# A routed two-layer kernel on one core: weight remainders on the matrix engine, a bf16 spreading product, and a token list stored as 16 rows

## The chip, the cores and the metric

The kernel runs on one core of a Trainium2 chip. The core's engines work side by side and meet at semaphores: TensorE (PE, matrix products into PSUM banks), VectorE (DVE), ScalarE (ACT), GpSimd (POOL), and SyncE (SP), which here only issues DMA transfers. Each engine takes its instructions in the order in which the program wrote them. The metric is the device time of one execution in microseconds.

## The reference, cut to what matters

```python
attn_out = _attn_ref(**attn_kwargs)            # banded local and global attention: B=4, H=8, S=544, D=64
x = attn_out.transpose(0, 2, 1, 3).reshape(B * S, H * D)      # 2176 tokens of 512
# routing: _moe_ref, E = 8 experts, cap = 2176 // 8 = 272
logits = x @ w_gate
order = np.argsort(-logits.flatten())
for idx in order:                              # the largest logit of all comes first
    tok, e = (int(idx) // E, int(idx) % E)
    if assigned[tok] >= 0 or counts[e] >= cap:
        continue
    assigned[tok] = e
    counts[e] += 1
for e in range(E):
    h = np.maximum(x[assigned == e] @ w1[e], 0.0)             # 512 -> 1024
    out[assigned == e] = h @ w2[e]                            # 1024 -> 512
# dense layer: _moe2_ref on all rows of out
h = x @ w_in                                                  # 512 -> 2048
P = a[0] + a[1] * h + a[2] * h**2 + a[3] * h**3
Q = 1.0 + np.abs(b[0]) * np.abs(h) + np.abs(b[1]) * h**2
return ((P / (Q + 1e-06)) @ w_out).astype(np.float32)         # 2048 -> 512
```

All tensors are float32 but w_in and w_out, which come as float64; the kernel reads those as pairs of 32-bit words and turns them into float32.

## The kernel before

The program has four kinds of work, and they overlap. First comes attention for the four batches, with the logits at its end; in between, the 32 pieces of 128x512 of w_in and w_out are loaded (SP) and turned into float32 (ScalarE and VectorE), all but the last four (NL), whose buffers come free later.

Then comes the routing, one turn for each expert. `search` finds the next expert that fills up: VectorE compares every token's best logit with 64 or 32 candidate thresholds (ind), TensorE counts (17 small bf16 products with oh), VectorE reduces the counts to one number per candidate (d), and TensorE spreads d over all 128 partitions by a product with an identity matrix, so that VectorE can choose the next candidates (nxt). This is done six times per expert (BITS) for seven experts; the eighth takes what is left. `members` then gives the chosen tokens slots, and two products (ha by rhs, spread by il) turn slots into a list of token numbers: il holds the list as 16 partitions of 17, idx as 128 partitions of 3. Before the change idx is also written to the DRAM tensor perm, 272 numbers of 4 bytes by three transfers. SP reads the expert's id (ei) into a register and loads the weights of this expert with it.

Third come the experts. GpSimd gathers the 272 rows of an expert from DRAM with three indirect transfers (t and p, later rows), TensorE transposes them, and ScalarE and VectorE split them into a high part, rounded to the fp32r format, and a low part, the remainder. All large products of the kernel are sums of three fp32r products (high by high, high by low, low by high, `mm3`). An expert's weights arrive in 16 loads of 256 KB (rows) and are split in the same way, the remainder by GpSimd, or for half of expert 0's by VectorE.

Last, the dense layer works on chunks of two or three blocks of 128 rows, 16 blocks of 128 hidden features each: `firsts` (into bank tq), `chain` (the quotient, on ScalarE and VectorE), `seconds` (into bank sc) and `store`, which reads the token numbers back from perm (ix) and writes the rows out with an indirect transfer. The dense weights need splitting once: `high` rounds a piece (ScalarE, whi_), and `low` makes the remainder (wlo_): two processes take pieces in turn, one on GpSimd, one on VectorE. Both begin as soon as the first piece is rounded, that is with the first routing.

The order on the engines is made at build time. Each piece of work is a generator that yields the engine and the time that it will hold it, or an event; the class Flow keeps a clock for each engine in a model and lets the process that can start first, or one of smaller rank shortly after, write its instructions next. The rank of `low` is 5 until the first expert is nearly there. Where TensorE would be idle before the first expert, `fill` writes products of ones by ones (`warm`), whose results nobody reads. So a change in one process moves the others as well.

Of the kernel before, what the change touches and what calls it, by code (L numbers as in the profile page):

```python
# [11 lines left out]
F32 = mybir.dt.float32  # L12
# [23 lines left out]
# turns a float64's high word, read as float32, into one whose exponent has float32's bias;  # L36
# what lies below 2^-119 becomes 0 or keeps below it
# [3 lines left out]
class Event:  # L41
    """Something that happens n times before the processes that wait for it go on."""
# [5 lines left out]
class Slots(Event):  # L48
    """n places, each taken by one process at a time."""
# [5 lines left out]
class Ring:  # L55
    """n buffers that are taken in turn. Who takes one gets the event of its release."""
# [9 lines left out]
class Flow:  # L66
    """The order in which the engines issue. A process is a generator; it yields (engine, time in us) and
    then traces the instructions that hold the engine for about that time, or yields an Event or Slots
    that it needs, or a time to pass; of a list of engines it gets the one that is free first, as
    self.engine. On a model of the engines' clocks the process that can start  # L70
    first goes on, or one of a smaller rank that follows shortly."""
# [75 lines left out]
    def free(self, e):  # L147
        """When an engine is free; the queue of the DMAs is kept short."""
        t = self.clock.get(e, 0.0)
        if e == "SP":  # L150
            queue = sum(p[3][0][1] for p in self.asks if p[3][0][0] == "DMA")
            t = max(t, self.clock.get("DMA", 0.0) + queue - QUEUE)
        return t
# [30 lines left out]
def moe_kernel(ctx: ExitStack, tc: tile.TileContext, q_l, k_l, v_l, q_g, k_g, v_g, w_gate, w1, w2,  # L184
               w_in, w_out, ca, cb, out, dbg=None):
    nc = tc.nc
# [29 lines left out]
    def warm(n, after=None):  # L216
        """Idle products: the array's clock stays up only while it is busy."""
# [12 lines left out]
    # 128 x 512 pieces of w_in (row block, column block) and of w_out (row block) in the order of use  # L230
# [14 lines left out]
    def load64(pool, i, v, bufs=2):  # L245
        """Steps that give a piece of a float64 tensor (its words as int32) as float32."""
# [10 lines left out]
    # ------------------------------------------------------------ attention  # L257
    vs, tail, tail_pe = [], [], []
    with ExitStack() as actx:
# [5 lines left out]
        # heads are taken in the order hh = 4 * (h % 2) + h // 2, pair pr holds hh = 2 pr and 2 pr + 1  # L265
# [9 lines left out]
        def copy(o, i):  # L275
            """A copy on the engine that the flow chose."""
            if flow.engine == "ACT":
                act(o, i, AF.Copy)
            else:
                V.tensor_copy(o, i)  # L280
# [14 lines left out]
        # band masks: partition (j, q), free (block of four, key)  # L295
# [9 lines left out]
        # dif[p, c] = key column - query in block, key column counted from the window's start  # L305
        nc.vector.tensor_scalar(dif, jq, pqf, -160.0, op0=OP.add, op1=OP.add)
        # keys lie in slots of 32, the global ones after every two blocks; a window of three blocks
        # and the global keys is four slots in a row, the global ones at place gp(its first block)
# [5 lines left out]
        def win(i):  # L314
            """The first block of the window of block i's queries."""
# [15 lines left out]
        # global q, k transposed: [(h2, d), pair, (b, s)]  # L331
# [24 lines left out]
        # ---- loads  # L356
# [22 lines left out]
        def load_two(src, b, r, slots, rows, name, ev):  # L379
            """256 rows, two neighbours in a partition."""  # L380
# [18 lines left out]
        def windows(b, half):  # L399
            """Window tiles: index n starts at key 32 n."""  # L400
# [34 lines left out]
        # ---- transposes of queries and keys  # L435
# [26 lines left out]
        def both_T(src, s, put, done, rank):  # L462
            """[(parity of the row, d), pair, row // 2] for each head of a pair."""
# [44 lines left out]
        def prep_q(b, r, rank):  # L508
            """Queries of eight blocks, block diagonal by head of a pair."""
# [11 lines left out]
        # ---- four blocks of 32 queries of all heads  # L521
# [32 lines left out]
        def tops_(u, ps, sc, A, mx, tops):  # L554
            # the scores and their largest, both times -scale
# [89 lines left out]
        def logits(XT, c):  # L645
# [9 lines left out]
            # [(j, e), tokens] -> [tokens, e], summed over j  # L655
# [8 lines left out]
        # ---- the 32 global queries of a batch against all 544 keys  # L664
# [119 lines left out]
        # ---- conversions of the dense layer's weights, between the others  # L784
# [53 lines left out]
    # ------------------------------------------------------------- routing  # L838
# [24 lines left out]
    ioi = rc.tile([128, 64], I32, name="ioi")  # L863
# [9 lines left out]
    # tri[p, m]: 1 for p < m, less 1 everywhere  # L873
    tri = rc.tile([128, 128], BF, name="tri")
    with tc.tile_pool(name="tmp", bufs=1) as tmp:
        wide = tmp.tile([128, 128], I32, name="wide")
        nc.gpsimd.iota(wide, pattern=[[1, 128]], base=0, channel_multiplier=0)
        widef = tmp.tile([128, 128], F32, name="widef")
        nc.vector.tensor_copy(widef, wide)
        nc.vector.tensor_scalar(tri, widef, pif, -1.0, op0=OP.is_gt, op1=OP.add)  # L880
    ones34 = rc.tile([128, 2 * NT], F32, name="ones34")
    nc.vector.memset(ones34, 1.0)
    # candidates: the first round's floats in sortable order, then bit patterns to flip
# [7 lines left out]
    # a float of 2^23 + v, v < 2^23, has the bits M23 + v: sums of steps give bit patterns  # L891
# [15 lines left out]
    # a one at column 128 - NS + p of partition p  # L907
# [3 lines left out]
    perm = dpool.tile([N, 1], I32, name="perm")  # L911

    # above every logit while a token is unassigned, then below every candidate
# [4 lines left out]
    # remaining places less a half  # L918
    REM = rc.tile([128, E], F32, name="REM")
    nc.vector.memset(REM, float(CAP) - 0.5)  # L920
    # tokens given to an expert so far | tokens tied at the threshold
# [710 lines left out]
```

## Time and the profile before

| | |
|---|---|
| time, median of 3 runs | 950.34 us (948.73 to 950.40) |
| span of the profiled execution | 948.0 us |
| busy: TensorE, VectorE, ScalarE, GpSimd | 856.5, 740.7, 498.9, 282.2 us |
| instructions | 20310 |

The span runs from the first instruction to the last one of the profiled execution; its own time outside the profiler is not among the three runs, whose median is 2.3 us above the span. Busy times of an engine are shares of the span and say nothing of where the engine was waited for; for this the span is cut into stretches, and the waits are read in each.

### The profile page before, as it was taken

How to read it: one execution, taken by the hardware profiler on the slowest of the kernel's cores; microseconds unless marked ns; L12 is line 12 of the kernel's file. 1: busy time of each engine (PE TensorE's matmuls, PEld its weight loads, DVE VectorE, ACT ScalarE, POOL GpSimd, SP SyncE). 2: the span in 40 equal slices, each digit the busy share in tenths (PEclk: the TensorE clock that was granted, in tenths of full speed). 3: DMA queues.
4: the chain of work that ended last, by engine and by line, in shares of the span. 5: the costliest groups of instructions: out<-in, count | busy, mean ns of one | idle time of the engine just before them, and what ended most of it. 6: DMA issues, size and time to landing. Idle time of an engine off the chain costs nothing.

```text
span 948.0 us, 20310 instructions
## 1 busy us (share of the span) xinstructions
PE 856.5 (90%) x7692; PEld 732.0 (77%) x7692; DVE 740.7 (78%) x1879; ACT 498.9 (53%) x1123; POOL 282.2 (30%) x229
## 2 busy tenths in 40 slices
PE   6879787856599699999999999999999999999997
PEld 4657665623279588888888889988899899899886
DVE  4657778889478498989879888988988757758985
ACT  5768867761043244554554455445455555646763
POOL 3111111055224132432434333252334343331001
PEclk8989888865779799999999999999999999999999
DMA  9999998620543421322122122212213313210000
GB/s 214 211 232 259 247 252 234 191 79 1 74 129 51 85 68 45 59 78 79 47 68 90 35 58 79 79 46 80 79 35 91 90 40 96 90 46 1 23 1 34
DMA packets 134194, 89.90 MB, mean 95 GB/s; under 512 B 31536, under 2 KB 122160, under 8 KB 134096
## 3 DMA queue, kind: packets, MB, share of 16 engines
q1 hardware_dynamic: 130672, 79.67, 32.3%
q0 software_dynamic: 2896, 8.92, 4.3%
q8 instruction: 60, 0.98, 0.6%
q14 instruction: 38, 0.31, 0.1%
q10 hardware_dynamic: 528, 0.02, 0.0%
HBM read 68.19 MB, written 8.92 MB: 81 GB/s over the span
## 4 chain that ended last, share of the span: by engine, by line
PE 62%; DVE 13%; issue 9%; DMA 9%; ACT 4%; SPq 2%; POOL 1%; POOLq 0%; DVEq 0%; ACTq 0%
PE sc L1174 7%; PE sc L1176 6%; PE sc L1175 6%; PE tq L1174 5%; PE sc L1179 5%; PE tq L1175 5%; PE tq L1176 5%; PE sc L1181 5%; PE sc L1180 5%; PE av L964 2%; PE sc L545 2%; DMA stg<-in_moe_w_out_dram 2%; DMA VW<-vr 1%; PE av L972 1%; DMA p<-xd,idx 1%
## 5 line engine op out<-in xcount | busy, mean ns | idle before, releaser
L1356 POOL TENSOR_TENSOR wlo<-rows,whi 128x512 fp32r<-128x512 f32 x120 | 174.3, 1454 | 368.4 <-ACT whi L1349 353.4
L1174 PE MATMUL tq<-yr,wh 128*128 128x256 f32 (+1 forms) x512 | 152.1, 297 | 1.4 <-DVE p L1493 1.4
L1175 PE MATMUL tq<-yr,wh 128*128 128x256 f32 (+1 forms) x512 | 148.8, 291 | 0.0
L1176 PE MATMUL tq<-yr,ws 128*128 128x256 f32 (+1 forms) x512 | 148.7, 290 | 0.0
L1174 PEld LDWEIGHTS tq<-yr,wh 128*128 128x128 f32 x512 | 97.4, 190 | 4.1 <-issue 2.1
L1179 PE MATMUL sc<-wh,t 128*128 128x512 f32 x248 | 99.7, 402 | 0.0
L1181 PE MATMUL sc<-wh,t 128*128 128x512 f32 x248 | 98.3, 397 | 0.4 <-DVE t L1521 0.4
L1175 PEld LDWEIGHTS tq<-yr,wh 128*128 128x128 f32 x512 | 97.6, 191 | 0.8
L1176 PEld LDWEIGHTS tq<-yr,ws 128*128 128x128 f32 x512 | 97.9, 191 | 0.0
L1180 PE MATMUL sc<-ws,t 128*128 128x512 f32 x248 | 97.6, 394 | 0.0
L1349 ACT ACTIVATE whi<-rows 128x512 fp32r<-128x512 f32 x120 | 75.5, 630 | 32.9 <-DMA rows<-in_moe_w_dram 25.3
L1388 ACT ACTIVATE hh<-sc 128x272 fp32r<-128x272 f32 x64 | 25.4, 396 | 118.5 <-PE sc L1176 118.3
L1481 ACT ACTIVATE t<-tq,coef 128x512 f32<-128x512 f32 (+1 forms) x67 | 44.8, 669 | 58.7 <-PE tq L1176 49.5
L1174 PE MATMUL sc<-xhi,whi 128*128 128x272 f32 x240 | 74.0, 308 | 0.0
L1174 PE MATMUL sc<-hh,whi 128*128 128x272 f32 x240 | 71.2, 296 | 0.0
L1176 PE MATMUL sc<-xhi,wlo 128*128 128x272 f32 x240 | 69.9, 291 | 0.0
L1175 PE MATMUL sc<-xlo,whi 128*128 128x272 f32 x240 | 69.7, 291 | 0.0
L1176 PE MATMUL sc<-hh,wlo 128*128 128x272 f32 x240 | 69.2, 288 | 0.0
L1175 PE MATMUL sc<-hl,whi 128*128 128x272 f32 x240 | 69.0, 288 | 0.0
L1499 DVE SCALAR_TENSOR_TENSOR t<-t,b 128x512 f32<-128x512 f32 (+1 forms) x67 | 50.8, 758 | 17.3 <-ACT t L1483 16.9
L1502 ACT ACTIVATE t<-t,cq 128x512 f32<-128x512 f32 (+1 forms) x67 | 47.3, 706 | 22.2 <-DVE t L1499 22.0
L1181 PEld LDWEIGHTS sc<-wh,t 128*128 128x128 f32 x248 | 46.5, 188 | 15.1 <-DVE t L1521 4.4
(289 smaller groups left out, 2191.1 us busy)
## 6 DMA issues: line engine op xcount, KB each, us to landing
rows<-in_moe_w_dram SPq DMA_DIRECT2D x128, 256.0 KB, 2.9
stg<-in_moe_w_in_dram SPq DMA_DIRECT2D x16, 512.0 KB, 4.9
stg<-in_moe_w_out_dram SPq DMA_DIRECT2D x16, 512.0 KB, 4.9
VW<-vr SPq DMA_DIRECT2D x24, 256.0 KB, 5.1
kr<-in_k_l_dram SPq DMA_DIRECT2D x8, 512.0 KB, 7.3
qr<-in_q_l_dram SPq DMA_DIRECT2D x8, 512.0 KB, 6.2
vr<-in_v_l_dram SPq DMA_DIRECT2D x16, 256.0 KB, 5.4
VW<-vr SPq DMA_DIRECT2D x32, 128.0 KB, 4.7
```

The lines of the kernel that those rows point to most:

```text
L1174: nc.tensor.matmul(ps, whi, xhi, start=first, stop=False)
L1175: nc.tensor.matmul(ps, whi, xlo, start=False, stop=False)
L1176: nc.tensor.matmul(ps, wlo, xhi, start=False, stop=last)
L1179: nc.tensor.matmul(ps, ghi, whi, start=first, stop=False)
L1180: nc.tensor.matmul(ps, ghi, wlo, start=False, stop=False)
L1181: nc.tensor.matmul(ps, glo, whi, start=False, stop=last)
L1349: nc.scalar.activation(hi, raw, AF.Copy)
L1356: (V if alt else nc.gpsimd).tensor_tensor(lo, raw, hi.bitcast(F32), op=OP.subtract)
L1388: nc.scalar.activation(hh, ph[:, :CAP], AF.Relu)
L1481: nc.scalar.activation(q, ph, AF.Abs, scale=b0)
L1499: V.scalar_tensor_tensor(q, r, b1, q, op0=OP.mult, op1=OP.add)
L1502: nc.scalar.activation(r, q, AF.Ln, bias=cq)
```

## The change

Three things are changed. First, until the first expert is known (the event routed[0]), the remainder of a dense piece is made by TensorE: an fp32 product of the identity by the float32 piece, and, added in the same PSUM bank, an fp32r product of the negative identity (neg) by the rounded piece; each piece takes two halves of 256 columns, and ScalarE copies the bank (tq) to the piece's buffer. The processes on GpSimd and VectorE wait for routed[0] and take what is left. Second, d is written as bf16 and the spreading product uses a bf16 identity (identb). Third, the token list goes to perm as 16 rows of 17 numbers per expert, made from il by one VectorE operation (pk) in the new `note`, by one transfer; routed[j] now fires ahead of it, and the store waits for noted[c]. The reading of perm follows the new layout. Besides, some constants of the routing lie in a pool that is given back.

```diff
+    identb = rc.tile([64, 64], BF, name="identb")
+    nc.vector.tensor_copy(identb, identf[:64, :64])
...
-    perm = dpool.tile([N, 1], I32, name="perm")
-
-    # above every logit while a token is unassigned, then below every candidate
+    perm = dpool.tile([NS, E * NA], I32, name="perm")
...
-            d = rw.tile([J, 1], F32, name="d")
+            d = rw.tile([J, 1], BF, name="d")
             yield "DVE", 0.09
             V.tensor_tensor_reduce(out=junk, in0=pc, in1=REM[:J], op0=OP.subtract, op1=OP.max, scale=1.0,
                                    scalar=-3.0e38, accum_out=d)
             yield "PE", 0.14
             pb = rps(128, J)
-            nc.tensor.matmul(pb, d.to_broadcast([J, 128]), identf[:J, :J], start=True, stop=True)
-            # the largest candidate that keeps d above 0, and the next ones from it
+            nc.tensor.matmul(pb, d.to_broadcast([J, 128]), identb[:J, :J], start=True, stop=True)
...
-        for c in range(NCH):
-            n = min(128, CAP - c * 128)
-            nc.sync.dma_start(dram(perm, j * CAP + c * 128, [[1, n], [1, 1]]), idx[:n, c:c + 1])
...
+        return il
+    def note(j, il):
+        yield "DVE", 0.08
+        pk = rw.tile([NS, NA], I32, name="pk", bufs=2)
+        V.scalar_tensor_tensor(pk, il[:, 0, :NA], 16.0, il[:, 1, :NA], op0=OP.mult, op1=OP.add)
+        nc.sync.dma_start(perm[:, j * NA:(j + 1) * NA], pk)
+        flow.fire(noted[j])
...
-        yield from members(j, est, j == E - 1)
-
-    # ------------------------------------------------- experts, then the dense layer on their rows
-    # Rows are taken in the order in which experts fill: the expert of turn j owns CAP positions
-    # from j * CAP on, the dense layer works on chunks of TW positions. The experts' outputs are in
-    # a ring of RB blocks of 128 positions, in two parts.
+        il = yield from members(j, est, j == E - 1)
+        flow.fire(routed[j])
+        yield from note(j, il)
...
+    def low_pe():
+        neg = mo.tile([128, 128], F32R, name="xhi", bufs=1)
+        nc.scalar.activation(neg, identf, AF.Copy, scale=-1.0)
+        while nlo[0] < NW64 and not routed[0].at:
+            yield lo_s
+            i, nlo[0] = nlo[0], nlo[0] + 1
+            yield hi_done[i]
+            yield tq_s
+            p = None
+            for h in range(2):
+                yield "PE", 0.65
+                p = bank("tq", 2) if p is None else p
+                o = slice(256 * h, 256 * h + 256)
+                nc.tensor.matmul(p[:, o], identf, vs[i][:, o], start=True, stop=False)
+                nc.tensor.matmul(p[:, o], neg, whi_[i][:, o], start=False, stop=True)
+            def out_(i, p):
+                yield "ACT", 0.6
+                wlo_[i] = wslot(F32R)
+                nc.scalar.activation(wlo_[i], p, AF.Copy)
+                flow.fire(tq_s)
+                flow.fire(lo_done[i])
+                flow.fire(lo_s)
+            flow.go(out_(i, p), 4)
     def low(eng, name, dur):
+        yield routed[0]
...
-            flow.fire(routed[j])
...
+        yield noted[c]
         yield rows_s
         yield "ACT", 0.48
         if c not in ixs:
             ixs[c] = mo.tile([128, 3], I32, name="ix", bufs=2)
             for h, blk in enumerate(BLK[c]):
-                nc.sync.dma_start(ixs[c][:, h:h + 1], dram(perm, blk * 128, [[1, 128], [1, 1]]))
+                nc.sync.dma_start(ixs[c][:, h:h + 1], dram(perm, blk * 128 // NS, [[1, 128 // NS], [E * NA, NS], [1, 1]]))
...
-        for gen, rank in ((router(), pace), (high(), 5), (last_pieces(), late), (low(nc.gpsimd, "POOL", 1.23), late),
+        for gen, rank in ((router(), pace), (high(), 5), (last_pieces(), late), (low_pe(), 5), (low(nc.gpsimd, "POOL", 1.23), late),
```

What this moves is seen at three places. The first is TensorE in the first routing, a round of 32 candidates: before, from the last counting product (av<-oh,ind) over the spreading product (av<-identf,d) to the next round's first.

```order
L964 MATMUL av<-oh,ind 32x8
L223 LDWEIGHTS onesb
L223 MATMUL sc<-onesb 128x512
L972 MATMUL av<-identf,d 128x32
L223 LDWEIGHTS onesb
L223 MATMUL sc<-onesb 128x512
L223 LDWEIGHTS onesb
L223 MATMUL sc<-onesb 128x512
L223 LDWEIGHTS onesb
L223 MATMUL sc<-onesb 128x512
L964 LDWEIGHTS ind
```

The same place after the change; tq<-ws,identf and tq<-wh,xhi are the two products of a half (xhi is the name of neg's buffer).

```order
L971 MATMUL av<-oh,ind 32x8
L1273 MATMUL tq<-ws,identf 128x256
L1274 MATMUL tq<-wh_3207,xhi 128x256
L979 LDWEIGHTS d
L979 MATMUL av<-identb,d 128x32
L1273 MATMUL tq<-ws,identf 128x256
L1274 MATMUL tq<-wh_3207,xhi 128x256
L1273 MATMUL tq<-ws,identf 128x256
L1274 MATMUL tq<-wh_3217,xhi 128x256
L1273 MATMUL tq<-ws,identf 128x256
L1274 MATMUL tq<-wh_3217,xhi 128x256
L971 LDWEIGHTS ind
```

In place of four filler products stand four halves, one ahead of the spreading product and three behind it; 46 halves (23 pieces) stand in the whole first routing, five ahead of the first count, 13 between the steps of `members`, and three behind them.

The second place is GpSimd at the start of the first routing and up to the second gather, before:

```order
L877 IOTA wide 128x128
L1252 TENSOR_TENSOR ws<-ws,wh_3116 128x512
...
L1252 TENSOR_TENSOR ws<-p,wh_3422 128x512
L1289 DMA t_3638<-xd,idx 128x512 x2
L1289 DMA p<-xd,idx 16x512
L1252 TENSOR_TENSOR ws<-p,wh_3614 128x512
L1356 TENSOR_TENSOR wlo<-rows,whi 128x512 x8
L1252 TENSOR_TENSOR ws<-p,wh_4324 128x512
L1289 DMA t_4382<-xd,idx 128x512 x2
```

And after, where ws is a dense remainder and wlo one of an expert's weights:

```order
L880 IOTA wide 128x128
L1332 DMA t_3655<-xd,idx 128x512 x2
L1332 DMA p<-xd,idx 16x512
L1296 TENSOR_TENSOR ws<-ws,wh_3500 128x512
L1399 TENSOR_TENSOR wlo<-rows,whi 128x512 x2
L1296 TENSOR_TENSOR ws<-ws,wh_3524 128x512
L1296 TENSOR_TENSOR ws<-p,wh_3559 128x512
L1399 TENSOR_TENSOR wlo<-rows,whi 128x512 x3
L1296 TENSOR_TENSOR ws<-p,wh_4011 128x512
L1399 TENSOR_TENSOR wlo<-rows,whi 128x512 x5
L1332 DMA t_4516<-xd,idx 128x512 x2
```

The 18 subtractions ahead of the first gather are gone, five stand behind it (four of them ahead of the second gather); on VectorE 11 are gone from the first routing and four stand behind it.

The third place is SP's queue at the end of the first routing, before:

```order
L249 DMA stg_3516<-in_moe_w_out_dram 128x1024
L1106 DMA perm<-idx 128x1 x2
L1106 DMA perm<-idx 16x1
L1322 TENSOR_LOAD ei
L1322 ISA x2
L1332 ISA
L1332 DMA rows<-in_moe_w_dram 128x4x128
```

And after:

```order
L251 DMA stg_3783<-in_moe_w_out_dram 128x1024
L1365 TENSOR_LOAD ei
L1365 ISA x2
L1128 DMA perm<-pk 16x17
L1375 ISA
L1375 DMA rows<-in_moe_w_dram 128x4x128
```

Three writes ahead of the reading of the id have become one behind it.

## Rows read from the trace of the kernel before

**Rows 1.** windows: stretch, length, busy PE, PEld, DVE, ACT, POOL, granted clock, DMA share, GB/s

```profile
311.50:319.40 7.90, 1.26 (x5) 0.64 (x6) 0.66 (x2) 1.40 (x3) 0.67 (x1) 0.69 0.67 170
...
319.40:340.00 20.60, 19.24 (x169) 16.65 (x170) 13.93 (x39) 9.71 (x20) 4.80 (x4) 0.79 0.18 52
...
420.00:500.00 80.00, 79.62 (x629) 71.44 (x626) 68.71 (x149) 39.65 (x72) 29.41 (x22) 1.00 0.23 67
```

**Rows 2.** windows, the same columns: two stretches of attention, one of the first routing

```profile
144.00:148.00 4.00, 4.00 (x52) 3.14 (x50) 3.97 (x24) 3.20 (x14) 0.00 (x0) 1.00 0.78 241
...
156.00:160.00 4.00, 4.00 (x35) 2.34 (x37) 3.16 (x9) 2.18 (x5) 0.00 (x0) 0.50 0.92 265
...
220.00:230.00 10.00, 6.61 (x53) 2.98 (x53) 9.42 (x18) 0.00 (x0) 8.12 (x5) 0.50 0.00 0
```

**Rows 3.** timeline, first routing: start, us, engine, line, operation

```profile
188.23 0.69 DVE L255 SCALAR_TENSOR_TENSOR ws<-stg,ws 128x512 int32<-128x512 int32 x1
...
195.06 5.90 POOL L1252 TENSOR_TENSOR ws<-ws,wh 128x512 fp32r<-128x512 f32 x4 [16.82 <-ACT wh L1164]
...
195.15 0.17 DVE L661 COPY LG<-tx 128x8 f32<-128x8 f32 x1 [1.35 <-PE tx L659]
...
207.03 1.19 DVE L987 TENSOR_TENSOR nxt<-low,flips 128x64 int32<-128x64 int32 x1
```

**Rows 4.** timeline of VectorE, second search

```profile
303.18 0.28 DVE L938 TENSOR_TENSOR lm<-LG,OPEN 128x136 f32<-128x136 f32 x1
...
309.95 0.23 DVE L987 TENSOR_TENSOR nxt<-low,flips 128x64 int32<-128x64 int32 x1
```

**Rows 5.** chain that ended last, in order of time: start, us, what

```profile
202.23 1.30 DVE ind L960
...
229.84 0.62 PE av L964 x17
...
232.72 1.20 DVE g L999
...
269.11 0.23 PE sc L1174
```

**Rows 6.** timeline, from the first expert's id to its gathered rows

```profile
245.16 0.14 DVE L1115 CAST ei<-ef 1x1 int32<-1x1 f32 x1
...
247.91 1.42 POOL L1289 DMA_INDIRECT p<-xd,idx  x1 [0.31 <-issue]
...
260.65 0.28 PE L1312 MATMUL tx<-identf,p 16*128 16x16 f32 x1 [2.34 <-DMA p<-xd,idx]
```

**Rows 7.** DMA issues of the whole span: count, KB each, median us to landing

```profile
rows<-in_moe_w_dram SPq DMA_DIRECT2D x128, 256.0 KB, 2.9
...
rows<-xd,idx POOLq DMA_INDIRECT x18, 3.5
```

**Rows 8.** DMA issues in 375 to 392 us

```profile
perm<-idx SPq DMA_DIRECT2D x2, 0.5 KB, 8.8
```

**Rows 9.** instructions by line: count, ns minimum/median/maximum, first and last start

```profile
L685 PE MATMUL sc<-KT,qgT x32: 592/643/1116, 35.1 to 169.6; 128*64 128x512 f32 x32
...
L1181 PE MATMUL sc<-wh,t x19: 388/392/498, 600.0 to 633.9; 128*128 128x512 f32 x19
```

**Rows 10.** timeline of TensorE around a spreading product and two bf16 products

```profile
420.66 0.40 PE L972 MATMUL av<-identf,d 32*128 32x32 f32 x2
...
421.00 0.39 PE L1174 MATMUL sc<-xhi,whi 128*128 128x272 f32 x1
...
440.36 0.19 PE L1043 MATMUL av<-mk,onesb 128*128 128x34 bf16 x1
...
440.42 0.37 PE L1174 MATMUL sc<-xhi,whi 128*128 128x272 f32 x1
```

**Rows 11.** timeline of TensorE, second list's spread and expert 1's first product

```profile
301.59 0.37 PE L1096 MATMUL av<-il,spread 16*128 16x6 bf16 x8
...
329.75 0.48 PE L1174 MATMUL sc<-xhi,whi 128*128 128x272 f32 x1
```

More of the change, by code (lines that the diff above doesn't have):

```diff
@@ L216, in warm @@
     def warm(n, after=None):
+        if n < 1:
+            return
         p = bank("sc", 4)
@@ L862, in moe_kernel @@
     nc.vector.tensor_copy(tpf, tpart)
-    ioi = rc.tile([128, 64], I32, name="ioi")
+    once = ExitStack()
+    ot = once.enter_context(tc.tile_pool(name="once", bufs=1))
+    ioi = ot.tile([128, 64], I32, name="ioi")
     nc.gpsimd.iota(ioi, pattern=[[1, 64]], base=0, channel_multiplier=0)
@@ L874, in moe_kernel @@
     tri = rc.tile([128, 128], BF, name="tri")
[L875 to L880, printed above, removed]
+    wide = ot.tile([128, 128], I32, name="wide")
+    nc.gpsimd.iota(wide, pattern=[[1, 128]], base=0, channel_multiplier=0)
+    widef = ot.tile([128, 128], F32, name="widef")
+    nc.vector.tensor_copy(widef, wide)
+    nc.vector.tensor_scalar(tri, widef, pif, -1.0, op0=OP.is_gt, op1=OP.add)
+    identb = rc.tile([64, 64], BF, name="identb")
+    nc.vector.tensor_copy(identb, identf[:64, :64])
     ones34 = rc.tile([128, 2 * NT], F32, name="ones34")
@@ L906, in moe_kernel @@
         flips.append(t)
+    once.close()
     spread = rc.tile([NS, 256 - NS], BF, name="spread")
@@ L1188, in moe_kernel @@
     routed = [Event() for _ in range(E)]
+    noted = [Event() for _ in range(E)]
     started = [Event() for _ in range(E)]
```

## The prediction

> **What bounds the kernel now.** I read the windows by stage first. From 340 us on TensorE is the bound: 79.62 of 80 us busy at a granted clock of 1.00 while VectorE has 68.71 [rows 1]. Work taken off TensorE there shortens the kernel, and whatever starts that stretch earlier moves the end one for one. Ahead of it lie two places where TensorE does not work for the result. One is the first routing, from the last logits at 195.3 us to the expert's id at 245.3 [rows 3, 6], followed by a wait until the first expert product at 269.11 [rows 5]. The other is a hole at 311.5 to 319.4 in which it is busy for 1.26 of 7.90 us [rows 1], waiting for the second gather. The change touches both, and the small product that stands in all searches.
>
> **First routing (term A).** The reader is to see in rows 3 and 4 what slows it: the same instruction, nxt of 128x64, takes 1.19 us while GpSimd subtracts (POOL, 195.06 and on) and 0.23 in the second search. The change takes all 18 GpSimd and 11 VectorE subtractions out of this stretch and puts 46 half pieces on TensorE instead, with 23 PSUM copies on ScalarE. The price of a half is not in the trace, so from the nearest rows: an fp32 instruction of 512 columns takes 592 ns, an fp32r one 388 [rows 9]. The difference of 204 is 512 more cycles at 2.4 GHz, so fp32 goes at two cycles a column and fp32r at one; an fp32 product is two instructions (32 records for 16 products). A half of 256 columns is then 0.43 + 0.11, some 0.55 us, and 1.1 us at 1.2 GHz. The order has four such halves in each round of 32 candidates, so TensorE and no longer VectorE sets the round: count 0.6 [rows 5], spreading product 0.2, halves 2.2, together 3.0 us. The two rounds of 64 candidates come to 3.8 and 3.4. Step by step:
> - logits to first candidates: seven operations which without GpSimd take some 0.3 us each, as lm's 0.28 at 303.18 [rows 4], and two conversions of 0.69 [rows 3]: 3.5 with the gaps, now 6.9 (195.3 to 202.2).
> - the six rounds: first scan 1.3, then 3.8 + 3.4 + 4 x 3.0: 20.5, now 30.5 (202.23 to 232.72, rows 5).
> - the tail to the id: thirteen halves of 0.55 between the router's own steps, 10.5 in all, now 12.6.
> The id is then known at 195.3 + 34.5 = 229.8, 15.5 us earlier. At 1.2 GHz throughout the rounds come to 36.2 and the tail to 17.5: 252.5, 7 us later than now. ScalarE hides the copies: 29 roundings and 23 copies at some 0.6 are 31 us of a 34 us stretch; if it fell behind, the two PSUM banks would hold TensorE by that much, a few us.
>
> Which clock? In 144 to 148 us TensorE, full of fp32 products into PSUM banks that other engines empty, was granted 1.00 [rows 2]; after an idle stretch it was 0.50 for 4 us of full work (156 to 160) and rose later; with filler at 66% busy it stayed at 0.50 (220 to 230). The halves stand without gaps, so I take 2.4 GHz after a first few slow us. The Trainium skill (TensorE: Matmul & The Clock Gate, "A second HAM failure mode: psum-queue depth-cycling") says against this that cycling through PSUM banks makes micro-idles in which the clock falls back. By that rule the id comes at 252.5 and the sum is 932, not 910; the row of 144 to 148 does not bear it out.
>
> **First gather (B).** The last part of the gathered rows is there at 260.65, 15.3 us after the id, although its issue came 2.6 us after it [rows 6]; gathers of the later experts land in 3.5 [rows 7]. What stands in the way are 272 writes of 4 bytes to perm: in 375 to 392 us, with only two weight loads and a gather beside it, such a write lands after 8.8 us [rows 8]. The change writes 16 runs of 68 bytes in one transfer, behind the reading of the id, and takes two issues out of SP's queue. On SP that write waits for pk, one VectorE operation after the id, and four weight loads stand behind it: 0.2 us, which the shorter queue pays. I put the landing at 2.6 + 3.5 and 1 for the weight loads (2.9 alone, rows 7) beside it: 7 after the id, 8 gained. The bounds are nothing (if loads and gather hold each other) and 9. The way from landing to first product, 8.5 us, I leave as it is. The Trainium skill (DMA: Bandwidth & Descriptors, "Latency and other measured facts") puts a DMA's fixed cost at about 2 us, mostly the receipt from HBM. By that rule perm is no obstacle in either form, B and C vanish, and the sum is 926; the 8.8 us speak against it.
>
> **Second gather (C).** The same writes precede it. From the spread of the second list at 301.59 to expert 1's first product at 329.75 are 28.2 us [rows 11], of which 6.6 are the idle time of the hole, and some 4 go to the half clock behind it (0.79 on the mean of 20.6 us, rows 1). The new order puts one more dense step and some second-layer products ahead of the transposes, but that step waits for a PSUM bank, and I charge 2.5 for it: 8 gained, between 3 and 10.
>
> **Spreading product in bf16 (D).** In the TensorE-bound part the fp32 product holds the stream for 0.34 us (420.66 to 421.00), while two bf16 products with their loads take 0.06 from the first start to the next work (440.36 to 440.42) [rows 10]. There are six in each of seven searches, 36 behind the first: 36 x 0.28 = 10. The bounds are 0 (nothing but the wait for d) and 10; I take 9, since VectorE, 86% busy, keeps some.
>
> **What costs nothing.** Nine subtractions are left for the time of expert 0 (GpSimd 5, VectorE 4; before, 3 in all); there TensorE is full, and that hides 4 x 0.7 us; without this cover up to 6 us. The packed list is one more VectorE operation of some 0.15 us per expert behind the id. The reads of perm stay 4 bytes each and are issued while the chunk's dense work has yet to begin, which hides them; without it each would cost about a landing, 3 us as a weight load's [rows 7]. The last weight piece is loaded one expert later, well before the last dense step of chunk 0 asks for it.
>
> **The sum.** 15.5 + 8 + 8 + 9 = 40.5 off the span of 948.0: 907.5. The median of the runs, 950.34, is 2.3 above the profiled span, so 910.
>
> **Rivals.**
> - The clock stays at 1.2 GHz in the routing: 932. For it: 220 to 230 at 0.50. Against: the filler there leaves gaps, the halves do not. Chance 0.15.
> - Weights and gather hold each other and the hole only moves: B and C give nothing, 926. For it: 0.25 MB a weight load, four at once; against: rows 8. Chance 0.15.
> - The bf16 product frees TensorE but VectorE takes its place: 919. For it: 68.71 of 80 us busy; against: 11 us are left in that window. Chance 0.13.
> - Slower: the clock stays low beyond the routing into expert 0. Then the id is 7 late, expert 0's 31 us of TensorE work take some 27 more, C is gone, B and D stay: 965. It turns slower than before from some 18 us lost, that is 36 us of the expert's time at half clock. For it: 0.50 in 156 to 160 under full load; against: it rose soon after. Chance 0.05.
> - Nothing changes, since the weights' loads set expert 0's start whatever the routing does: 949. Against: TensorE's wait named the gather. Chance 0.03.
> The forecast itself has 0.49, with a range of its own from 902 to 918.
>
> **Numbers.** The range is 902 to 932, which leaves out little but the last two rivals and the far ends. Runs of this kernel differ by 0.2%, which is what can be told from no change: faster by more 0.93, within 0.02, slower 0.05.
>
> **What would show it.** A: ei at 228 to 232 us, nxt of 128x64 at 0.23, granted clock 1.00 from about 200 on, rounds of 3 us. If the halves last 1.1 us and the clock reads 0.50, A is wrong. B: perm landing in some 3 us, the gathered rows within 7 of the id, first expert product near 245. C: no stretch of 5 us without TensorE between the experts. D: the spreading product as one record, and 340 to 900 us of old work done in some 8 us less. If TensorE's busy share falls below 97% there, another engine has become the bound and D is wrong.

## The result, and the profile after

The changed kernel takes 935.13 us (median of 4 runs, 932.87 to 936.45) against 949.54 for the kernel before, a ratio of 0.9844 with a 95% interval of 0.982 to 0.9868. It is faster, by some 15 us where 40 were forecast. The profiled span is 931.1 us against 948.0, so 16.9 less.

First the early part. Timeline of the changed kernel: start, duration, engine, line, operation, and in brackets the idle time before it with what ended it.

```profile
203.68 0.23 DVE L994 TENSOR_TENSOR nxt<-low,flips 128x64 int32<-128x64 int32 x1
204.07 0.60 PE L1273 MATMUL tq<-ws,identf 128*128 128x256 f32 x2
204.62 0.60 PE L1273 MATMUL tq<-ws,identf 128*128 128x256 f32 x2
...
231.39 0.14 DVE L1119 CAST ei<-ef 1x1 int32<-1x1 f32 x1
...
234.71 0.93 POOL L1332 DMA_INDIRECT p<-xd,idx  x1 [0.30 <-issue]
...
239.36 0.69 DVE L1399 TENSOR_TENSOR t<-rows,t 128x512 fp32r<-128x512 f32 x1 [3.85 <-ACT t L1392]
...
240.18 0.23 PE L979 MATMUL av<-identb,d 64*128 64x64 bf16 x1 [3.99 <-DVE d L975]
240.36 0.19 PEld L1355 LDWEIGHTS tx<-identf,t 128*128 128x128 f32 x1
...
247.89 0.60 PE L1189 MATMUL sc<-xhi,whi 128*128 128x272 f32 x1
```

The reader sees nxt at the 0.23 us of [rows 4] instead of the 1.19 of [rows 3], halves at a pitch of 0.55 us, the first id at 231.39 (245.16 before, [rows 6]) and the first expert product at 247.89. By the same timeline that product stood at 268.54 before (the chain's piece in [rows 5] begins inside it, at 269.11). So the experts start 20.65 us earlier. The clock, in windows of both kinds of stretch (busy time of PE, PEld, DVE, ACT and POOL with instructions, then the granted clock, DMA share and GB/s):

```profile
196.00:200.00 4.00, 3.07 (x10) 2.62 (x10) 2.75 (x7) 3.51 (x7) 0.00 (x0) 0.50 0.45 135
204.00:230.00 26.00, 25.91 (x233) 21.02 (x231) 14.93 (x64) 21.72 (x40) 0.00 (x0) 1.00 0.06 21
248.00:252.00 4.00, 4.00 (x17) 3.69 (x18) 2.23 (x9) 0.52 (x2) 0.00 (x0) 0.50 0.14 56
264.00:268.00 4.00, 4.00 (x34) 3.79 (x31) 3.27 (x10) 1.45 (x4) 1.28 (x1) 0.72 0.27 80
296.00:300.00 4.00, 3.06 (x25) 2.46 (x26) 3.06 (x11) 0.00 (x0) 1.80 (x2) 0.56 0.67 205
344.00:348.00 4.00, 4.00 (x15) 3.28 (x14) 3.84 (x7) 3.40 (x8) 0.10 (x1) 0.57 0.07 20
```

In the routing the halves hold 2.4 GHz for 26 us at 25.91 us busy. Behind it TensorE is granted 1.2 GHz four times for 3 to 14 us, each time after it had waited.

Where the rest went shows when both kernels are cut at the same events: first product of experts 0, 1, 3 and 6, and the end. Kernel before, then the changed one:

```profile
268.54:329.75 61.21, 53.09 (x463) 47.66 (x461) 39.51 (x120) 18.77 (x39) 16.42 (x12) 0.85 0.36 78
329.75:487.50 157.75, 153.24 (x1235) 137.34 (x1233) 138.33 (x299) 76.51 (x145) 55.33 (x42) 1.00 0.23 62
487.50:730.09 242.59, 241.20 (x1925) 217.63 (x1923) 212.79 (x468) 123.21 (x228) 90.62 (x69) 1.00 0.23 66
730.09:948.00 217.91, 209.88 (x1303) 191.48 (x1301) 159.15 (x260) 121.66 (x231) 54.45 (x51) 1.00 0.17 49
```

```profile
247.89:311.81 63.92, 58.13 (x512) 50.32 (x510) 49.47 (x143) 22.33 (x44) 15.27 (x12) 0.89 0.25 73
311.81:468.42 156.61, 147.95 (x1175) 132.85 (x1174) 136.36 (x287) 74.58 (x142) 57.61 (x43) 0.99 0.22 65
468.42:711.69 243.27, 240.38 (x1915) 214.72 (x1913) 216.23 (x473) 124.16 (x228) 86.94 (x69) 1.00 0.22 66
711.69:931.10 219.41, 209.92 (x1298) 190.25 (x1296) 164.50 (x259) 122.61 (x231) 55.81 (x51) 0.99 0.16 48
```

From the first product on the changed kernel needs 683.2 us, 3.7 more than before (679.5), though its TensorE has 36 cheaper products. The stages do not hold quite the same work (512 products instead of 463 in the first), since the planner, which makes the order at build time, moved some. Its idle time (length less PE busy) is 26.8 us instead of 22.1: 5.8 against 8.1 in the first stage, 21.0 against 14.0 behind it. In the three longest waits between 311.81 and 900 VectorE is full (5.97 of 6 us in 326 to 327, 340 to 343 and 406 to 408). Around the longest one, timeline of VectorE:

```profile
324.97 1.77 DVE L1564 TENSOR_TENSOR t<-t 128x512 fp32r<-128x512 f32 x1
...
340.94 1.77 DVE L1088 TENSOR_TENSOR rhs<-hk,tpf 128x289 bf16<-128x289 bf16 x2
342.63 0.68 DVE L1564 TENSOR_TENSOR t<-t 128x512 fp32r<-128x512 f32 x1
```

The same operation (L1564) takes 0.68 us at 342.63 and 1.77 at 324.97, while GpSimd subtracts (POOL wlo at 324.78 and 340.48, 1.41 and 1.54 us); in 340 to 344 TensorE is busy for 1.49 of 4 us. And the second expert's gather, on which C rests:

```profile
286.67 0.14 DVE L1119 CAST ei<-ef 1x1 int32<-1x1 f32 x1
...
290.10 0.69 DVE L1296 TENSOR_TENSOR ws<-p,wh 128x512 fp32r<-128x512 f32 x1
...
291.88 2.88 POOL L1399 TENSOR_TENSOR wlo<-rows,whi 128x512 fp32r<-128x512 f32 x2 [14.82 <-ACT whi L1392]
...
294.90 0.98 POOL L1332 DMA_INDIRECT t<-xd,idx  x1
...
296.28 0.94 PE L971 MATMUL av<-oh,ind 128*64 128x8 bf16 x17 [2.45 <-DVE ind L967]
```

It is issued 8.2 us after the id. GpSimd stood idle for 14.8 us ahead of two weight remainders, and the gather is written behind them. It goes into the buffer t1, which late weight pieces use as well; the subtraction of a late piece (ws<-p) at 290.10 is, by the code, what lets one go; an experiment below takes that up.

### The profile page after: what moved, and what is told of

It reads as the page before. It is cut to its first block, busy times and chain, and to the rows that moved or that the text cites. A ratio compares the mean times of both kernels' runs of the same rounds, so it can differ in the third digit from the quotient of the medians.

```text
span 931.1 us, 20363 instructions
## 1 busy us (share of the span) xinstructions
PE 852.1 (92%) x7727; PEld 733.6 (79%) x7727; DVE 735.0 (79%) x1880; ACT 513.9 (55%) x1147; POOL 256.2 (28%) x214
## 4 chain that ended last, share of the span: by engine, by line
PE 53%; DVE 24%; issue 9%; DMA 7%; ACT 5%; SPq 2%; POOL 0%; DVEq 0%; POOLq 0%; ACTq 0%
PE sc L1189 5%; PE tq L1189 5%; PE sc L1191 4%; PE sc L1190 4%; PE sc L1196 4%; PE sc L1194 4%; PE tq L1190 4%; PE tq L1191 4%; PE sc L1195 4%; DVE t L1560 3%; DVE t L1562 3%; PE tq L1273 2%; PE av L971 2%; DMA stg<-in_moe_w_out_dram 2%; DVE t L1542 2%
## 5 line engine op out<-in xcount | busy, mean ns | idle before, releaser
L1196 PE MATMUL sc<-wh,t 128*128 128x512 f32 x248 | 99.8, 403 | 2.7 <-DVE t L1564 2.3
L1194 PE MATMUL sc<-wh,t 128*128 128x512 f32 x248 | 100.3, 405 | 0.0
L1191 PEld LDWEIGHTS tq<-yr,ws 128*128 128x128 f32 x512 | 97.7, 191 | 0.0
L1542 DVE SCALAR_TENSOR_TENSOR t<-t,b 128x512 f32<-128x512 f32 (+1 forms) x67 | 55.9, 834 | 21.1 <-ACT t L1526 20.8
```

Of the source, the lines that this page charges most:

```text
L1191: nc.tensor.matmul(ps, wlo, xhi, start=False, stop=last)
L1194: nc.tensor.matmul(ps, ghi, whi, start=first, stop=False)
L1196: nc.tensor.matmul(ps, glo, whi, start=False, stop=last)
L1542: V.scalar_tensor_tensor(q, r, b1, q, op0=OP.mult, op1=OP.add)
```

## The experiments

Ratios are to the kernel before, run on the same chip. Differences between two kernels are taken between their ratios, times 949.5 us; they are uncertain by some 3 us.

**One part alone, one part out.** Two theories were set against each other: V, that behind the routing VectorE, stretched by GpSimd, is the bound, so that TensorE time set free becomes waiting; and T, that the bf16 product brings its full price and the order of instructions lost the rest. `after_fp32_spread` and `before_bf16_spread` change

```diff
-nc.tensor.matmul(pb, d.to_broadcast([J, 128]), identf[:J, :J], ...)   # d fp32
+nc.tensor.matmul(pb, d.to_broadcast([J, 128]), identb[:J, :J], ...)   # d bf16
```

in one direction or the other. `before_pe_low` is the kernel before with low_pe() and the wait of low() for routed[0]; `before_list16` has note(), the 16 rows and noted; `list16_bf16` has all but low_pe(). Those of these that are made from the kernel before also give back the pool of routing constants, as the changed kernel does.

> The changed kernel with the spreading product in fp32 again; every engine's order is that of the changed kernel. Theory V (behind the first routing VectorE is the bound, slowed by GpSimd, so TensorE time that is freed there becomes waiting): 935 to 938 us. Rival T (the bf16 product brings its 0.3 us in each of 36 places, and what is missing was lost to the order that the planner made): 944 to 947 us, idle time of TensorE behind expert 1's first product as now, 21 us.

> The kernel before with the spreading product alone in bf16. TensorE's idle time there is only 14 us behind expert 1's first product. Theory V: at most 4 us gained, 945 to 950. Rival T: 938 to 941.

> The kernel before with only the low parts made on TensorE until the first expert is known. Both theories: the id some 14 us earlier, first expert product 12 to 14 earlier. Theory V: about half of it reaches the end, 940 to 944. Rival T: all of it does, 935 to 938.

> The kernel before with only the token list as 16 rows, written behind the id. Both theories: first expert product 7 us earlier, the id where it was. Theory V: 943 to 946 at the end. Rival T: 935 to 940, since the second gather comes early as well.

Measured: 940.97 us (0.9896, 0.9872 to 0.992), 942.39 (0.9909, 0.9891 to 0.9927), 944.45 (0.9935, 0.9917 to 0.9953) and 943.9 (0.9932, 0.9911 to 0.9953). Alone, the bf16 product brings 8.6 us, TensorE's 6.2 and the list's 6.5; the bf16 product on top of the other two brings 4.9. So neither V nor T holds as written. The bf16 product arrives whole in the kernel before and, as far as 3 us of uncertainty can tell, by half in the changed one. The early starts give about what V said (943.9 lies in its range, 944.45 just above it), but the traces show another reason. Expert 1's first product comes 10.3 us earlier in `before_pe_low` and 10.5 in `before_list16` (table below), the end only 4.6 and 5.6. What is lost in between is about what the clock takes: in `before_list16` TensorE, back at work behind the second gather, stays at half clock for some 20 us.

```profile
307.00:328.00 21.00, 20.72 (x138) 17.53 (x139) 10.68 (x31) 7.62 (x16) 3.43 (x3) 0.51 0.16 44
```

Counted as under "The clock" below, the loss at half clock is 13.1 us in `before_list16` and 12.7 in `before_pe_low`, against 7.5 in the kernel before.

The next expectations use names that are explained further below: theory C is that the clock takes back what the early start brought, theory G that late weight pieces hold the buffer of the second gather.

In `after_write4` the transfer has its old form, three DMAs of 4-byte writes in note()'s place, and the compute engines' orders are those of the changed kernel:

```diff
-nc.sync.dma_start(perm[:, j * NA:(j + 1) * NA], pk)
+for c in range(NCH):
+    n = min(128, CAP - c * 128)
+    nc.sync.dma_start(dram(perm, j * CAP + c * 128, [[1, n], [1, 1]]), ready[j][0][:n, c:c + 1])
```

> The changed kernel with the 272 writes of 4 bytes for each expert in place of the 16 runs, issued as in the kernel before; the order of all compute instructions is that of the changed kernel. Both theories have the first gathered rows 7 us later. If all of it reached the end: 942. By theory C half of it is made up, since the later start runs at a higher clock: 937 to 940. Rival W (the weights end last now, so the list costs nothing): 934 to 936.

> The changed kernel without its first part: the low parts on GpSimd and VectorE from the start, as in the kernel before. If the three parts add up: 935 + 6 = 941 us. By theory G the part on TensorE gives back what it brings, since it leaves the late pieces until after the id: 932 to 936, as fast as the changed kernel.

Measured: 949.14 us (0.9993, 0.9975 to 1.0011) and 937.59 (0.9891, 0.9872 to 0.991). The list is worth 14 us in the changed kernel, more than anything expected here, and since only the form of the writes differs, it is the form that costs this: the first product comes 23.1 us after the id instead of 16.5, and the second gather is issued 13.7 after its id instead of 8.2. Rival W is out. The part on TensorE adds 4.5 us to the other two; alone it gave 6.2, which is the same within the uncertainty. 937.59 lies between the two expectations, 936 and 941.

**The clock (theory C).** `after_fill` lets the idle products that the planner writes into TensorE's gaps fill them whole, and until the second expert's time; 39 more products, nothing else moves.

```diff
-FL, FM, SR = 0.45, 0.7, 0.1
+FL, FM, SR = 1.0, 1.0, 0.1
-if front["e"] >= 0 or xs_ and gap < 0.5:
+if front["e"] >= 1 or xs_ and gap < 0.5:
```

> The changed kernel with 39 more idle products in the planner's gaps of TensorE until the second expert's time; the order of all other instructions is the same. Theory C (what the early start brought is given back in stretches at 1.2 GHz that follow TensorE's short waits between the first expert product and 350 us; 8.5 us of work at full clock are lost so): granted clock up at 240 to 252 and 296 to 303, 4 us gained, 930 to 932 us. Theory V (VectorE, slowed by GpSimd, sets these stretches): no change, 934 to 937, since the clock only moves the waiting.

Measured 929.86 us (0.9794, 0.9768 to 0.982), some 4.7 us gained, as C expects. Its windows:

```profile
248.00:252.00 4.00, 4.00 (x48) 3.62 (x46) 2.94 (x12) 1.48 (x3) 0.70 (x1) 1.00 0.21 80
...
296.00:300.00 4.00, 4.00 (x44) 3.56 (x45) 3.48 (x11) 0.00 (x0) 0.00 (x0) 1.00 0.12 41
```

The clock is up where it was down. From the first product on TensorE loses 8.5 us to it in the changed kernel (busy time times what the granted clock lacks to 1.00, summed over windows of 1 us) and 3.3 here. In the kernel before it loses 7.5, so the clock is a cost of both kernels and explains little of what the changed kernel lacks, other than in the two kernels with one early start alone.

**GpSimd's remainders of the expert weights (theory V).** Three kernels leave them out, and with them the buffer wlo; every other compute instruction stands where it stood:

```diff
-(V if alt else nc.gpsimd).tensor_tensor(lo, raw, hi.bitcast(F32), op=OP.subtract)
+if alt:
+    V.tensor_tensor(lo, raw, hi.bitcast(F32), op=OP.subtract)
+else:
+    lo = hi
```

> The changed kernel without GpSimd's remainders of the expert weights (the rounded part is used in their place, so this part of the computation is left out); every other instruction stands where it stood. Theory V: VectorE no longer stretched by 1.1 us now and then, idle time of TensorE behind the first expert product from 27 to under 15 us, 918 to 924 us. Theory C: the stretches at 1.2 GHz stay, 930 to 935.

> The kernel before without GpSimd's remainders of the expert weights (the rounded part is used in their place, so this part of the computation is left out), all other instructions where they stood. Theory V (it is in the changed kernel that VectorE, stretched by GpSimd, takes the place of TensorE): at most 15 us gained here against 28 there, 934 to 940 us. Rival: it costs the same in both, 920 to 924, and so does not explain what is missing.

> All 28 pieces in hand on TensorE, and without GpSimd's remainders of the expert weights (the rounded part is used in their place, so this part of the computation is left out). Theory V (GpSimd's remainders hold TensorE up through VectorE, and all the more the earlier the experts start): the same floor as the changed kernel without them, 905 to 909 us, so 13 to 16 gained. If the two costs were apart: 28 gained again, 893 us.

Measured: 907.31 us (0.956, 0.9532 to 0.9588), 938.18 (0.9884, 0.9866 to 0.9903) and 907.91 (0.9566, 0.9544 to 0.9587). The remainders cost 11 us in the kernel before, 27 in the changed one and 14 in the next experiment's kernel, and the last two meet at the same floor, as V expects. The 27 us are more than V gave: 907.31 lies 11 us below its range, while the other two lie in theirs. Without these remainders the change brings 31 us (0.956 against 0.9884) instead of 15. VectorE in the changed kernel without them, in the second and third of the stages above, and the shares of the chain of waits over the whole span (kernel before, changed, changed without remainders, one line from each page):

```profile
309.33:454.59 145.26, 144.53 (x1175) 131.44 (x1174) 114.47 (x287) 74.17 (x142) 9.91 (x12) 1.00 0.23 70
454.59:692.30 237.71, 237.71 (x1915) 214.90 (x1913) 187.51 (x473) 123.29 (x228) 16.50 (x21) 1.00 0.23 67
```

```profile
PE 62%; DVE 13%; issue 9%; DMA 9%; ACT 4%; SPq 2%; POOL 1%; POOLq 0%; DVEq 0%; ACTq 0%
```

```profile
PE 53%; DVE 24%; issue 9%; DMA 7%; ACT 5%; SPq 2%; POOL 0%; DVEq 0%; POOLq 0%; ACTq 0%
```

```profile
PE 65%; issue 15%; DMA 8%; DVE 5%; SPq 3%; ACT 3%; POOL 1%; POOLq 0%; DVEq 0%; ACTq 0%
```

The same 287 VectorE instructions take 136.36 us with GpSimd at work and 114.47 without; TensorE's idle time in that stage goes from 8.66 to 0.73. VectorE's share of the chain had doubled with the change, from 13 to 24%. GpSimd's own share of the chain is 1% or less in all three, so it costs through the others. These kernels also free the weights' buffers some 1.3 us sooner a piece, so not all of the 27 us need be VectorE's; how much is the one and how much the other was not tested.

**The nine subtractions.** In `after_pe_all_held` TensorE goes on until the 28 pieces in hand are done, and GpSimd and VectorE get the four late ones:

```diff
-while nlo[0] < NW64 and not routed[0].at:
+while nlo[0] < NW0:
```

with an event at its end, for which low() waits in place of routed[0], and the negated identity in a place of YR (the buffer of the experts' outputs) that is still free.

> The changed kernel, where TensorE goes on with the low parts until all 28 pieces in hand are done, so that GpSimd and VectorE get only the four late ones. Theory V: five subtractions less beside expert 0, 2 to 4 us gained, 931 to 933. Theory C: TensorE is busier where it waited, but the low parts of 1.1 us each push the second search: 933 to 938.

Measured 921.53 us (0.9711, 0.9685 to 0.9736): 12.6 us below the changed kernel, three times what was expected or more. First product at 248.50, as before it, but the second gather goes out with its id, and expert 1 begins 14 us earlier, at 297.39:

```profile
282.34 0.99 POOL L1334 DMA_INDIRECT t<-xd,idx  x1 [7.31 <-DVE ef L1116]
282.35 0.14 DVE L1119 CAST ei<-ef 1x1 int32<-1x1 f32 x1
```

That made theory G: the nine subtractions cost by holding the second gather's buffer, against O: by their time on the two engines. `after_late_first` takes them in another order; `after_gather_first` leaves their order and reserves the buffer:

```diff
 for j in range(E):                    # gather()
+    if j == 1:
+        yield t1_s
     yield routed[j]
...
-    for s in [t1_s] if early else [rows_s] * NCH:
+    for s in [] if j == 1 else [t1_s] if early else [rows_s] * NCH:
```

> The changed kernel with the same nine subtractions left to GpSimd and VectorE, but three of the four late pieces taken ahead of four of the five that are in hand, so that the buffer which the late pieces share with the second gather is free sooner; in the new order the second gather follows the last late piece on GpSimd directly. Theory G (what the list should bring for expert 1 is lost because that gather's buffer is held by the late pieces until 290.8 and it then stands behind two remainders on GpSimd): second gather issued within 2 us of the second id, expert 1's first product 8 to 12 us earlier than in the changed kernel, 922 to 927 us. Theory O (the nine subtractions cost by the time they take on VectorE and GpSimd): 933 to 937.

> The changed kernel, nine subtractions left as they were, but the second gather takes its buffer right behind the first gather, so that no late weight piece can hold it. Theory G (the held gather is what the nine subtractions cost): gather within 1 us of the second id, expert 1's first product 7 us earlier after that id (25 to 18 us), 925 to 928 us at the end. Rival O (what costs is VectorE and GpSimd being busy with the nine beside expert 0): the gather is early but the end stays at 933 to 937.

Measured: 928.12 us (0.9782, 0.9767 to 0.9797) and 929.04 (0.9793, 0.9766 to 0.982). In `after_late_first` the gather still went out 9.4 us after the id (298.57 against 289.17), behind the last late piece's subtraction, so its 5.9 us do not come from the gather and it doesn't tell G from O. It lies between the two expectations, and it shows that expert 1's start does not by itself set the end: there expert 1 begins at 318.13, 6.3 us later than in the changed kernel, with more other work done ahead of it (540 products instead of 512). In `after_gather_first` it goes with the id (286.75), expert 1's first product follows 19.1 us after that id instead of 25.1, and 4.8 us reach the end. So G carries some 5 of the 12.6 us, give or take 3. The others may be O's kind: the second id comes at 286.75 with the nine subtractions and at 282.35 without five of them. That is read from two traces and not isolated, and the order on TensorE differs too: between the first products of experts 0 and 1 it has 512 products in the changed kernel, 449 in `after_gather_first` and 433 in `after_pe_all_held`.

> All 28 pieces in hand on TensorE and the full filler of the run after_fill. Theory C: the 8 us that are still lost at 1.2 GHz shrink, 917 to 919 us. If the gather alone was the matter: 921 to 923.

The fastest kernel that computes everything: `after_pe_all_held` with the fill of above takes 920.34 us (0.97, 0.9677 to 0.9723), between the two expectations. The filler adds nothing certain here (0.9711 without it), although the loss at half clock falls from 8.3 to 0.9 us. Both beat the changed kernel and the kernel before.

| us of the span | first id | first product | second id | second gather | expert 1's first product | end |
|---|---|---|---|---|---|---|
| before | 245.16 | 268.54 | 303.11 | 303.10 | 329.75 | 948.0 |
| before_pe_low | 233.06 | 257.82 | 295.50 | 295.50 | 319.42 | 943.4 |
| before_list16 | 244.49 | 260.18 | 299.09 | 299.09 | 319.25 | 942.4 |
| after | 231.39 | 247.89 | 286.67 | 294.90 | 311.81 | 931.1 |
| after_late_first | 233.99 | 250.35 | 289.17 | 298.57 | 318.13 | 927.5 |
| after_gather_first | 231.54 | 247.91 | 286.75 | 286.75 | 305.84 | 926.6 |
| after_pe_all_held | 230.81 | 248.50 | 282.35 | 282.34 | 297.39 | 920.2 |

## Why the prediction was wrong

Too much was promised, 40.5 us where the span gave 16.9. The table above says where the 23.6 us are missing: 1.7 up to the first id, 1.1 from there to the first product, 4.2 from there to the second id, 6.5 from there to expert 1's first product, and 10 behind it, where the changed kernel needs 619.3 us against 618.2 although D had promised 9 less. This is a place in time and not yet a cause, as the stages hold somewhat different work. By the prediction's steps:

**A (15.5), right and a little large.** The id came 13.8 us earlier. Pitch of the halves, nxt, the clock and the rounds (3.2 us instead of 3.0) were as said. Most of what was missing went ahead of the first count, at 201.35 where the sum gives 200.1: it stood behind five half pieces, the first of them at 0.50, and the "first few slow us" had no term. The rival of a routing at 1.2 GHz is out. So is, here, the rule of the Trainium skill (TensorE: Matmul & The Clock Gate, "A second HAM failure mode: psum-queue depth-cycling"): the halves cycle through two PSUM banks and the clock reads 1.00.

**B (8), right.** From id to first product 16.5 us instead of 23.4, so 6.9. The last part of the gather was issued at 234.71, and the same part of the second gather lands after 2.8 us; by that the rows are there some 6 us after the id, within the 7 that were said. The landing itself, and that of the write to perm, are not in the trace. The way from there was left as it is at 8.5 us and took some 10: the transposes stand behind a spreading product of the second search, whose d waited on VectorE behind a weight remainder (239.36). `after_write4` prices the list at 14 us, which B and C together put at 16. The rival that weights and gather hold each other anyway is out, and with it the sum that follows from the Trainium skill's fixed cost of 2 us (DMA: Bandwidth & Descriptors, "Latency and other measured facts"): the list's form would then have changed nothing.

**C (8), lost in this kernel.** From the second id to expert 1's first product it is 26.6 us before, 25.1 in the changed kernel, 20.2 with the list alone and 15.0 in `after_pe_all_held` (where less other work stands in between). The forecast, 20 from the list's spread and so 18.5 from the id, is near where the gather goes out with its id; here it waited 8.2 us. The sign that was named, no stretch of 5 us without TensorE between the experts, came true all the same: the longest wait there is 2.45 us. But the some 4 us at half clock, which were to go with the hole, stayed: after the short wait the clock is 0.50 from 296.5 to 303.3 us.

**D (9), right in size, in part not paid out.** Alone it gives 8.6 us, in the changed kernel 4.9. The sign that was named for another engine as the bound, a busy share of TensorE below 97% in 340 to 900 us, did not come. Kernel before, then the changed one:

```profile
340.00:900.00 560.00, 553.66 (x4167) 502.40 (x4164) 467.57 (x939) 291.52 (x547) 194.39 (x155) 1.00 0.22 63
340.00:900.00 560.00, 547.07 (x4048) 492.18 (x4048) 470.98 (x921) 293.22 (x546) 184.15 (x149) 1.00 0.20 60
```

The share falls from 98.9 to 97.7%. In the shorter stage of 311.81 to 468.42 it is 94.5% (147.95 of 156.61): the mean over the long stretch hid it. So the rival "frees TensorE but VectorE takes its place", which had 0.13, is true in part, and 11 us of VectorE time left in [rows 1] were its counter-argument. That average hid that VectorE's time is stretched by GpSimd: 21.9 us of the 136 in one stage are not there when GpSimd's remainders are left out.

**"What costs nothing", the step that failed.** It put the nine subtractions left for the time of expert 0 at nothing, and at most at 6 us. `after_pe_all_held`, which takes five of them away, is 12.6 us faster. What is shown of the reason is the buffer: the late pieces wait behind those in hand, and they share t1 with the second gather. "The last weight piece is loaded one expert later, well before the last dense step of chunk 0 asks for it" looked at the dense step and not at the buffer (5 us, `after_gather_first`). The rest is open. From the first id to the second it is 55.3 us in the changed kernel, 51.5 in `after_pe_all_held` and, with all nine subtractions but without GpSimd's remainders of the expert weights, 51.9; so VectorE and GpSimd have a part in it, but the order on TensorE differs as well. With all pieces in hand on TensorE the part is worth 17 us on top of the other two (0.9711 against 0.9891), near A's own figure; as it was made, 4.5.

**Left out of the sum: GpSimd against VectorE.** D kept 1 us of 10 for a busy VectorE, and nothing stands for GpSimd beside it. Without GpSimd's remainders the changed kernel runs at 907.31 us. The kernel before loses 11 us to them, this one 27. Of the 23.6 us between forecast and span the 16 us by which this loss grew are the most. That it grew because an earlier start and a lighter TensorE leave fewer waits in which VectorE can catch up is an argument; the runs show the two sizes. What it grew by and what the nine subtractions cost overlap, since both vanish at the same floor (907.31 and 907.91).

**"Moves the end one for one", too simple.** The prediction took it that whatever starts the TensorE-bound stretch earlier moves the end by as much. In `before_pe_low` and `before_list16`, where each early start stands alone, half of it was lost, about as much as the longer stay at half clock takes; in `after_late_first` a later start of expert 1 went with an earlier end.

One sum mixes two measures: the slower rival's 965 is a span, while the other rivals are medians of runs, by which it would be 967.

Open is how the part of the nine subtractions that is not the gather's splits between VectorE's time, GpSimd's and the order on TensorE, and how much of the 27 us comes from buffers that are free sooner.

## What to carry to other kernels

Before work is called hidden, follow every buffer that it holds to the next one who asks for it, on all queues: here late weight pieces kept the gather of another process back for 8 us. When an early wait is removed, ask which engine was catching up during it: it can become the bound further on, and its busy share, averaged over a long stretch, does not tell. Try whether one engine can take over a piece of work whole: here 28 pieces on TensorE were worth 17 us, 23 of them 4.5. And do not count a time at half clock as gone with the wait ahead of it.

## What the runs showed of the hardware

- A VectorE subtraction with both inputs in SBUF takes longer beside one of GpSimd: 1.77 us instead of 0.68 for one of 128x512. The Trainium skill (SBUF — State Buffer, "SBUF: two separate sides") says that VectorE and GpSimd share a pair of ports which one holds for a whole instruction; the stretch of 1.1 us against GpSimd's 1.4 agrees. What GpSimd's remainders of the expert weights cost at the end went from 11 to 27 us with nothing changed in them.
- In the changed kernel waits of TensorE of 1 to 3 us between the experts were followed by 3 to 7 us at 1.2 GHz (0.50 in the records: 265 to 269, 296 to 303, 344 to 347 us), though not every one: the wait of 1.3 us at 406 was not. In `before_list16` a wait of 1.7 us that ended at 307.28 was followed by 20 us at 1.2 GHz, in which TensorE was busy almost throughout. 26 us of products without gaps through two PSUM banks ran at 2.4 GHz.
- Of the 272 writes of 4 bytes, the transfer with the last 16 landed after 10.1 us in `after_write4` beside the weights' loads (225 to 310 us), and the same list as 16 runs made the kernel 14 us faster.
